# One store one slot later, and q in two transfers of 64 partitions instead of four of 32

## The chip, the cores and the metric

The kernel runs on one core of one Trainium2 chip. The metric is the device time of one execution in microseconds (us); less is better. The core has a matrix engine (TensorE, PE in the profile, with its weight loads shown as PEld), a vector engine (VectorE, DVE), a scalar engine (ScalarE, ACT), GpSimd (POOL) and SyncE (SP). SP computes nothing here: it issues nearly all of the DMA transfers, one after the other in the order in which the program lists them. Sixteen DMA engines carry the transfers between HBM and the on-chip memory of 128 partitions.

## The reference

Eight batches of eight heads; each head has 576 positions of 64 numbers in float32. Attention without a softmax is followed by a two-layer network with a leaky ReLU:

```
kv  = einsum('bhsd,bhse->bhde', k, v)
out = einsum('bhsd,bhde->bhse', q, kv)
rms = sqrt(mean(out * out, axis=-1) + 1e-6)
x   = (out / rms * g_norm)             # transposed to 4608 tokens x 512
h   = x @ w_in                         # 512 x 2048
g   = max(0.01 * h, h)
out = g @ w_out                        # 2048 x 512, result 4608 x 512
```

## The kernel before, in words

The 4608 tokens are worked on as nine blocks of 512 (`NB = 9`, block 0 to block 8). The 2048 inner columns are cut into four parts (`NC = 4`), and two parts next to each other make a pair: the second product is run by pairs. Both products of the network are done with Strassen's recursion in one to three levels, so that the matrix engine multiplies fewer blocks and the other engines add and subtract blocks. The sums of the weights are made once, written to HBM and read back for every block: `read` (L801) fetches one of seven pieces of a part of the first weights into a ring of five places, `read_side` (L1031) the right sides of the second product into three places, and `load_four`, `load_three` and `load_last_3` (L992 to L1017) the smaller ones.

From block 1 on the program is written out by slots. A block has 28 slots, seven for each part (`for t in range(7)`, L1446), and `tick` counts them through all blocks. In each slot the program issues one step of the first product, one step of the second product, which lags behind by two slots, and bits of the attention of the next batch by tables (`FINE_SLOTS` and its like). Work that has been put off by `put_off(n, ...)` is issued at the start of the slot n later (L1449). `pin` keeps instructions in program order on their engine, so SP's order is the order of the calls. A DMA in SP's order that has to wait holds up all that SP would issue after it.

q comes in by `load_pair` (L158), for the two heads of a pair p in batch b. A head is read as 32 rows of 18 positions, `T * D` = 1152 numbers. It is put into the tile twice: on partitions 64l to 64l+31 as it is, and on partitions 64l+32 to 64l+63 shifted by 32 numbers (`src[:, 32 * c:]`), where l is 0 or 1 for the two heads. So a pair takes four transfers of 32 partitions. `turn` (L511) then transposes, by blocks of 32 x 32, the first 32 of every 64 columns, which gives q with the head dimension on the partitions (L513, on DVE). The tile for q has one home from batch 3 on (and two before, one of them in w_all), so the load of the next pair is issued right after the transpose of the pair before it: `turn` and then `load_q`, which puts the next load at the head of `to_load`. Batch 0 has its own path (`load_first`), so there are 28 pairs, 7 batches of 4, with 112 transfers at L172.

The result of a block is held in four tiles of 256 x 256, with the keys "11", "12", "21" and "22" by token half and column half. Each is added up over the two pairs of parts and stored when its last sum has been issued; that happens while the next block has begun. `store` (L1308) puts the store off by two slots, the store of "12" by one slot if `tick > 14 * NC`, that is from slot 57 on, which is the case for blocks 2 to 6. In the last blocks the stores go through ACT's queue without being put off. The home of "12" of one block is that of "11" of the next, which is first written by a copy in the second step of the next block's first pair.

The lines of q's transfers as they stand:

```
for c in range(2):
    r0, n = 64 * l + 32 * c, T * D - 32 * c
    src = q[b, 2 * p + half_of(p, l)].rearrange("(t s) d -> t (s d)", s=T)
    pin(nc.sync.dma_start(t[r0:r0 + 32, :n], src[:, 32 * c:]))
```

Of the kernel before, what the change touches and what calls it, by code (L numbers as in the profile page):

```python
# [24 lines left out]
def kernel(  # L25
# [36 lines left out]
    nc = tc.nc  # L62
    B, H, S, D = q.shape
# [6 lines left out]
    T = S // 32  # L70
# [4 lines left out]
    NC = DF // 2 // (U * P)  # L75
# [17 lines left out]
    pin = tc.keep_in_program_order  # L93
# [32 lines left out]
    def half_of(p, i):  # L126


        return i ^ (p & 1)

    def load_two(eng, src, t):

        pin(eng.dma_start(t.rearrange("p j d -> p (j d)"),
                          src.rearrange("h (p j) d -> (h p) (j d)", j=J)))
        return t

    def in_tile(name):
        return ins.tile([P, J, D], F32, tag=f"{name}_in", name=f"{name}_in")

    def q_tile(b, p):  # L140
        if p % 2 and NP * b + p < NP * 3 + 2:
            return w1_all[:, 2 * NC * NW:]
        return ins.tile([P, T * D], F32, tag="q_in", name="q_in", bufs=1)
# [3 lines left out]
    def load_some(n=1):  # L147

        while to_load and n > 0:
            b, p, what = to_load.popleft()  # L150
            load_pair(b, p, what)
            n -= 1
# [5 lines left out]
    def load_pair(b, p, what="kvq"):  # L158


        if "k" in what:
            k_ins[b, p] = load_two(nc.sync, k[b, 2 * p:2 * p + 2], in_tile("k"))
        if "v" in what:
            v_ins[b, p] = load_two(nc.sync, v[b, 2 * p:2 * p + 2], in_tile("v"))
        if "q" not in what:
            return
        t = q_tile(b, p)
        for l in range(2):
            for c in range(2):
                r0, n = 64 * l + 32 * c, T * D - 32 * c  # L170
                src = q[b, 2 * p + half_of(p, l)].rearrange("(t s) d -> t (s d)", s=T)
                pin(nc.sync.dma_start(t[r0:r0 + 32, :n], src[:, 32 * c:]))  # L172
        q_ins[b, p] = t

    def load_first():
# [329 lines left out]
    def attention(b, apart=True, fine=False):  # L505
# [17 lines left out]
        for m in range(2):  # L523
            turn(2 * m)
            load_q(2 * m)
            yield
            turn(2 * m + 1)
            load_q(2 * m + 1)
            if m or b == KV_BESIDE:
                yield  # L530
            if kv_ps:
                attention_kv(b, m, [t[:, m, :] for t in kv_ps])
            if not apart and m == 0:
                for p in (2, 3):
                    load_pair(b, p)
            elif apart and not beside:
                load_kv(b + m, 2 - 2 * m)
            yield
            if apart:
                if m and kv_ps:  # L540
                    copy_kv(b, kv_ps)
                yield
# [147 lines left out]
    later, tick = [], 0  # L690

    def put_off(n, what):
        later.append((tick + n, what))
        later.sort(key=lambda x: x[0])
# [613 lines left out]
    def store(i):  # L1308
        def finish(key, o, part=None, cols=None, eng=None):
            r0 = i * NT + (int(key[0]) - 1) * N2  # L1310
            c0 = (int(key[1]) - 1) * N2
            if part is not None:
                r0 += part * P
                eng.dma_start(out[r0:r0 + P, c0 + cols.start:c0 + cols.stop], o[:, part, cols])
                return
            to = out[r0:r0 + N2, c0:c0 + N2].rearrange("(t p) m -> p t m", p=P)
            if steady and tick < 7 * (END - NC):
                put_off(1 if key == "12" and tick > 14 * NC else 2, lambda: pin(nc.sync.dma_start(to, o)))
            else:
                nc.scalar.dma_start(to, o)  # L1320
        return finish
# [49 lines left out]
    def between(n, half):  # L1371
        nonlocal loaded, rounded
        go(steps.get(2 * n + half, iter(())), 1)

        while half and rounded < min(3 * n + 8, 2 * n + 13, len(w_jobs) - (n < 11)):
            if loaded < len(w_jobs):
                load_w(loaded)
                loaded += 1
                if loaded in (15, 19):
                    load_pair(1, (loaded - 15) // 4)  # L1380
            round_w(rounded)
            rounded += 1
        if (n, half) == (12, 0):
            for p in range(2):
                load_pair(2, p)
# [192 lines left out]
```

## Time and profile before

| what | value |
|---|---|
| median of three executions | 908.37 us (908.33 to 910.28) |
| profiled execution, its own time | 909.21 us |
| its span in the profile | 907.5 us, TensorE at the full granted clock (1.0) |
| PE busy | 899.6 us, 99% |
| PEld / DVE / POOL / ACT busy | 789.3 / 611.9 / 521.8 / 330.5 us |
| DMA | 219.00 MB, mean 241 GB/s, 76.4% of the engines' span on SP's queue |
| transfers issued | 706 by SP, 18 by ACT, 8 by GpSimd |

The times are those of the slowest core, of which there is one. The profile counts an engine as busy from the start of an instruction to its end; the ends of matmuls are modelled. In the table of waits a wait for several signals is put down to the one that came last. A group's line gives the source line, the engine, the operation, the tile that is written and the tile that is read. DMA share is the time that the packets took, as a share of sixteen engines' time in that stretch; beside the views, the trace keeps a record of each packet with its start, its duration and its bytes, and of each completion signal.

### The profile page before, as it was taken

How to read it: one execution, taken by the hardware profiler on the slowest of the kernel's cores; microseconds unless marked ns; L12 is line 12 of the kernel's file. 1: busy time of each engine (PE TensorE's matmuls, PEld its weight loads, DVE VectorE, ACT ScalarE, POOL GpSimd, SP SyncE). 2: the span in 40 equal slices, each digit the busy share in tenths (PEclk: the TensorE clock that was granted, in tenths of full speed). 3: DMA queues.
4: the chain of work that ended last, by engine and by line, in shares of the span. 5: the costliest groups of instructions: out<-in, count | busy, mean ns of one | idle time of the engine just before them, and what ended most of it. 6: DMA issues, size and time to landing. Idle time of an engine off the chain costs nothing.

```text
span 907.5 us, 19134 instructions
## 1 busy us (share of the span) xinstructions
PE 899.6 (99%) x7344; PEld 789.3 (87%) x7344; DVE 611.9 (67%) x942; ACT 330.5 (36%) x645; POOL 521.8 (58%) x672
## 2 busy tenths in 40 slices
PE   8999999999999999999999999999999999999998
PEld 4555558888998999999999999999999999999997
DVE  5877885676574757685877497667877674646453
ACT  5454423231334332434333433343243424232420
POOL 2000236977638765766757584758477847883730
PEclk9999999999999999999999999999999999999999
DMA  8999918977789788967897798958886778677831
GB/s 253 225 248 235 249 66 264 312 255 247 246 298 323 220 276 251 310 225 249 259 321 267 221 296 253 323 171 270 257 277 187 229 210 274 199 237 226 259 115 53
DMA packets 109530, 219.00 MB, mean 241 GB/s; under 512 B 11776, under 2 KB 51072, under 8 KB 109440
## 3 DMA queue, kind: packets, MB, share of 16 engines
q1 hardware_dynamic: 105504, 212.22, 76.4%
q10 hardware_dynamic: 3488, 4.39, 1.4%
q8 instruction: 58, 0.95, 0.5%
q0 software_dynamic: 448, 1.18, 0.3%
q14 instruction: 32, 0.26, 0.1%
HBM read 187.34 MB, written 30.41 MB: 240 GB/s over the span
## 4 chain that ended last, share of the span: by engine, by line
PE 94%; POOL 2%; DMA 2%; DVE 1%; issue 1%; ACT 0%; POOLq 0%; ACTq 0%; DVEq 0%
PE o_a L121 19%; PE o_c L121 15%; PE h_hd L121 9%; PE h_ha L121 9%; PE h_hc L121 9%; PE h_hb L121 9%; PE o_acc L121 6%; PE h_ps L121 6%; PE o_ps L121 3%; PE h_a L121 2%; PE h_b L121 2%; PE kv_ps L121 1%; PE h_d L121 1%; PE h_c L121 1%; DMA pairs<-in_v_dram 1%; POOL more L697 1%
## 5 line engine op out<-in xcount | busy, mean ns | idle before, releaser
L697 POOL TENSOR_TENSOR gs<-g 128x512 f32<-128x512 f32 x62 | 85.5, 1380 | 129.4 <-ACT g L892 64.0
L121 PE MATMUL o_a<-pairs,gs 128*128 128x256 f32 x472 | 111.9, 380 | 0.7 <-DMA pairs<-w 0.7
L697 DVE TENSOR_TENSOR o_all<-o_c,o_all 128x256 f32<-128x256 f32 (+2 forms) x124 | 69.4, 560 | 59.1 <-PE o_c L121 45.7
L892 ACT ACTIVATE g<-g 128x512 f32<-128x512 f32 x124 | 75.7, 631 | 63.0 <-DVE g L697 63.0
L697 POOL TENSOR_TENSOR w_all<-w_all 128x512 f32<-128x512 f32 x28 | 50.2, 1793 | 84.0 <-ACT w_all L1116 84.0
L697 DVE TENSOR_TENSOR g<-g,w_all 128x512 f32<-128x512 f32 (+1 forms) x84 | 88.5, 1054 | 14.6 <-POOL w_all L697 8.8
L121 PEld LDWEIGHTS o_a<-pairs,gs 128*128 128x128 f32 x472 | 85.5, 190 | 10.4 <-POOL more L697 0.9
L697 DVE TENSOR_TENSOR w_all<-h_ha,w_all 128x512 f32<-128x512 f32 x42 | 28.7, 684 | 55.0 <-PE h_ha L121 53.2
L1116 ACT COPY w_all<-h_hc 128x512 f32<-128x512 f32 x42 | 24.8, 590 | 105.6 <-PE h_hc L121 105.4
L1116 ACT COPY w_all<-h_ha 128x512 f32<-128x512 f32 x42 | 24.7, 587 | 104.5 <-PE h_ha L121 104.5
L121 PE MATMUL o_c<-pairs,gs 128*128 128x256 f32 x264 | 62.4, 379 | 0.0
L697 DVE TENSOR_TENSOR o_all<-o_a,o_all 128x512 f32<-128x512 f32 (+1 forms) x53 | 35.4, 668 | 39.3 <-PE o_a L121 38.7
L697 POOL TENSOR_TENSOR pairs<-w 128x512 f32<-128x512 f32 x4 | 5.3, 1324 | 98.2 <-ACT cut L262 98.2
L121 PE MATMUL o_a<-w,g 128*128 128x256 f32 x248 | 58.9, 380 | 0.0
L121 PE MATMUL h_ps<-xT,w_all 128*128 128x512 f32 (+1 forms) x136 | 58.1, 571 | 0.3 <-DVE w_all L278 0.3
L121 PE MATMUL o_acc<-w,g 128*128 128x256 f32 (+1 forms) x192 | 57.7, 451 | 0.0
L121 PEld LDWEIGHTS o_acc<-w,g 128*128 128x128 f32 x192 | 36.3, 190 | 21.5 <-issue 17.2
L697 DVE TENSOR_TENSOR g<-w_all 128x1024 f32<-128x1024 f32 x28 | 34.7, 1238 | 29.4 <-ACT w_all L1116 29.4
L121 PEld LDWEIGHTS o_c<-pairs,gs 128*128 128x128 f32 x264 | 47.9, 190 | 5.3
L121 PEld LDWEIGHTS o_a<-w,g 128*128 128x128 f32 x248 | 45.0, 190 | 5.2 <-ACT xT L473 0.2
L121 PEld LDWEIGHTS h_ps<-xT,w_all 128*128 128x128 f32 x136 | 25.4, 190 | 26.9 <-issue 24.4
L121 PE MATMUL h_hc<-stage,w_all 128*128 128x128 f32 x336 | 44.9, 276 | 0.0
(291 smaller groups left out, 2403.4 us busy)
## 6 DMA issues: line engine op xcount, KB each, us to landing
w_all<-w SPq DMA_DIRECT2D x196, 448.0 KB, 4.8
pairs<-w SPq DMA_DIRECT2D x94, 256.0 KB, 4.4
w<-w SPq DMA_DIRECT2D x22, 448.0 KB, 5.9
v_in<-in_v_dram SPq DMA_DIRECT2D x29, 288.0 KB, 6.0
k_in<-in_k_dram SPq DMA_DIRECT2D x28, 288.0 KB, 5.4
q_in<-in_q_dram SPq DMA_DIRECT2D x46, 144.0 KB, 5.3
q_in<-in_q_dram SPq DMA_DIRECT2D x46, 140.0 KB, 5.4
w<-stage SPq DMA_DIRECT2D x12, 512.0 KB, 4.2
```

What stands on the lines that cost most here:

```text
L121: pin(nc.tensor.matmul(*args, **kw))
L697: ins = eng.tensor_tensor(out_, a, b_, op=ALU.subtract if minus else ALU.add)
L892: nc.scalar.activation(t, t if src is None else src, func=AF.Prelu, alpha=SLOPE)
L1116: nc.scalar.copy(q[:, at], bank)
```

## The change

In `load_pair` the loop over c goes. Each head is read by one transfer into 64 partitions. Its source is written out by hand as three dimensions: two copies that start 32 numbers apart, 32 rows that are 1152 numbers apart, and 1120 numbers in a row. The first copy is 32 columns shorter than before; those columns are not among the ones that the transpose reads. In `store` the condition goes: all stores that are put off are put off by two slots.

```
         t = q_tile(b, p)
+        n = T * D - 32
         for l in range(2):
-            for c in range(2):
-                r0, n = 64 * l + 32 * c, T * D - 32 * c
-                src = q[b, 2 * p + half_of(p, l)].rearrange("(t s) d -> t (s d)", s=T)
-                pin(nc.sync.dma_start(t[r0:r0 + 32, :n], src[:, 32 * c:]))
+            head = q[b, 2 * p + half_of(p, l)]
+            src = bass.AP(head.tensor, head.offset, [[32, 2], [T * D, 32], [1, n]])
+            pin(nc.sync.dma_start(t[64 * l:64 * l + 64, :n], src))
         q_ins[b, p] = t
...
             if steady and tick < 7 * (END - NC):
-                put_off(1 if key == "12" and tick > 14 * NC else 2, lambda: pin(nc.sync.dma_start(to, o)))
+                put_off(2, lambda: pin(nc.sync.dma_start(to, o)))
             else:
                 nc.scalar.dma_start(to, o)
```

## The prediction

> **What bounds the kernel now.** I read the page's busy times first, then the table of stretches, then the waits of the matrix engine, then those of SP.
>
> ```profile
> PE 899.6 (99%) x7344; PEld 789.3 (87%) x7344; DVE 611.9 (67%) x942; ACT 330.5 (36%) x645; POOL 521.8 (58%) x672
> PEclk9999999999999999999999999999999999999999
> q1 hardware_dynamic: 105504, 212.22, 76.4%
> q_in<-in_q_dram SPq DMA_DIRECT2D x46, 144.0 KB, 5.3
> q_in<-in_q_dram SPq DMA_DIRECT2D x46, 140.0 KB, 5.4
> ```
>
> PE is busy for 899.6 of 907.5 us at the full clock; 7.9 us are all that it idles. In the lines of transfers the last number is the median time from issue to landing. The next table gives, for each stretch, its length, the busy time of each engine, the clock, the DMA share and GB/s.
>
> ```profile
> 0.00:46.00 46.00, 42.66 (x386) 23.06 (x387) 31.41 (x65) 24.33 (x42) 5.18 (x14) 1.00 0.98 239
> 46.00:650.00 604.00, 603.05 (x5025) 524.91 (x5024) 426.49 (x659) 222.88 (x447) 362.06 (x455) 1.00 0.83 255
> 650.00:900.00 250.00, 249.98 (x1913) 237.83 (x1912) 152.27 (x214) 83.32 (x158) 154.59 (x203) 1.00 0.67 215
> ```
>
> All of the change's q loads lie between 46.1 and 647.4 us. There PE idles 1 us in 604, while the sixteen DMA engines are already busy for 0.83 of the time. So PE bounds this stretch, and DMA is the next in line, with 17% to spare. PE's own waits, and two of SP's, with total, times and longest in us:
>
> ```profile
> PE o_a L121 <- DMA pairs<-w: 0.7, 1, 0.7
> SPq L1318 <- DVE o_all L697: 21.0, 4, 5.5
> SPq L801 <- DMA w_all<-w: 4.1, 7, 0.8
> ```
>
> PE waits once for a weight, for 0.7 us. SP waits often, but nothing that matters waits for SP. The last view is time on SP and DVE in one block (start, duration).
>
> ```profile
> 442.45 1.25 DVE L513 STREAM_TRANSPOSE qT<-q_in 128x576 f32<-128x576 f32 x1
> 443.73 1.72 SPq L172 DMA_DIRECT2D q_in<-in_q_dram  x4
> 451.00 0.41 SPq L1318 DMA_DIRECT2D out_dram<-o_all  x1
> 451.48 1.25 DVE L513 STREAM_TRANSPOSE qT<-q_in 128x576 f32<-128x576 f32 x1
> 453.05 1.99 SPq L172 DMA_DIRECT2D q_in<-in_q_dram  x4
> 465.80 1.26 DVE L513 STREAM_TRANSPOSE qT<-q_in 128x576 f32<-128x576 f32 x1
> ```
>
> A pair's q is asked for right after the transpose before it, and the next transpose needs it 7.75 us (443.73 to 451.48) or 12.75 us (453.05 to 465.80) later; the first of the block's three such gaps is 9.5 us (432.98 to 442.45). In this program order DVE can do nothing else while it waits for q.
>
> **The store.** Five stores of "12" (blocks 2 to 6) are issued one slot later; a slot is about 3.4 us (a block of 96 us by 28). Their wait is the 21.0 us above: four waits, the longest 5.5, the one in the view ending at 451.00. Asked for a slot later, each should wait some 2 us, and the two reads queued behind it leave some 3.4 us earlier, 14 us of SP's time over all. PE does not wait for those reads now, so this gives 0; at the best it is the 1 us that PE idles in the stretch. It also costs nothing: the data isn't there sooner, and the home is next written in the second step of the following pair, six slots (some 20 us) after the last sum is issued, while two slots, a wait of 2 us and 5.6 us to landing make 14.5. What covers it is that distance; if a store took 11 us to land, ACT's copy of "11" would wait.
>
> **The issues.** 112 DMAs become 56. Four issues take 1.72 to 1.99 us on SP, so a pair saves some 0.9 us, 28 pairs 25 us of SP's time. It lies beside PE's work: 0. The bytes fall by 56 x 32 x 128 = 0.23 MB of 219: 0.
>
> **How the q transfers are spread.** This decides. Now each of the 112 transfers has 32 rows as its slowest dimension on both sides, all others 32 or 128. The trace has 11,712 completion signals for 732 transfers, 16 for each: all sixteen engines take part in every one. The new source has 2 as its slowest dimension, and no transfer of the trace has so small a one. So the cost is unknown and lies between two ends. If the rows still go out over sixteen engines, nothing changes. If a transfer is cut along its slowest dimension, it can only be cut in two, and two engines carry all of q. I take two: that every first dimension here is a multiple of sixteen, and every transfer signals sixteen times, fits a cut along that dimension, and such a cut of 2 gives two parts. It is not shown.
>
> [...]
>
> **The sum with two engines.** The packet records show q as 3,584 rows of 4,480 or 4,608 bytes, one packet each, together 64 us of each engine. In the stretch an engine is busy 0.83 x 604 = 501 us; without q that leaves 437. After the change each of the two carries half of q, 28 pairs x 2 transfers x 32 rows = 1,792 rows. The 4,480-byte packets took 173 ns undisturbed (the fastest 5%), 231 ns at the lower quartile, 293 ns at the median; 3,584-byte packets of 128-partition reads took 140 at the median, so something slows the rows of q.
> - At 173: 437 + 310 = 747 us, 143 more than the stretch.
> - At 231: 437 + 414 = 851, 247 more.
> - At 293: 437 + 525 = 962, 358 more.
> The two engines would then be the bound: every read of weights has an eighth of its rows on them, in turn behind q, and the ring's five places hold some 17 us of slots. I take 231: it is midway between undisturbed and today's median, as only two engines write q at once, though each to rows 32 partitions from the other's. Against the profiled execution: 909.2 + 247 = 1156; that execution lies 0.84 us above the median of 908.37, so against the median it is 1155. I say 1156.
>
> The bounds go further. If the other rows shrink to their undisturbed durations too, since fourteen engines will idle and contend less (by size, the fastest 5%: some 345 us in place of 437), 173 gives 655, or 51 more: 960. If two rows in turn share one way in, a row takes twice 173 = 346 ns: 437 + 620 = 1057, or 453 more: 1362.
>
> [...]
>
> **What is late next.** Whoever waits first is DVE at a transpose: two transfers are 64 rows on each engine, 11.1 us (173) to 18.8 (293), and some 2 us from issue to the first packet, against 9.5, 7.75 and 12.75 us. Behind the transpose stand DVE's additions from PE's banks, so PE stops for a free bank. On SP, transfers take eight completion signals in turn, so a late q also holds up the eighth transfer after it.
>
> **The rivals.**
> A, forecast: two engines carry q and are the bound. 1156, between 1040 and 1290. For it: 0.83 already used. Against it: no transfer shown with a slowest dimension of 2.
> B, late only: two engines, but rows near 173 and others quicker, so that throughput is not the bound and only transposes are late, by 13.1 - 9.5, 13.1 - 7.75 and 13.1 - 12.75, 9.3 us a block. Over six blocks 56 us, with a second queue of reads behind it up to 120: 965 to 1030, say 990. Against it: three q loads in 34 us of a block ask 33 us of these engines, on top of 0.8 of other reads.
> C, not slower: the spread stays at sixteen, as both sides have 64 rows in all. Then nothing in PE's chain moves: 908.4, within 1 us. For it: the same bytes now land in 5.3 us with sixteen signals. It decides from the first transfer on.
> D, faster: SP's 14 + 25 us let reads leave earlier and the 4 or 5 us of PE's start and waits shrink: 905. Against it: 3.3 of the 7.9 idle us are in the first 46 us and 3.6 at the end, which the change does not touch.
>
> **How the numbers follow.** A 0.66, B 0.19, C 0.12, D 0.03. The time is A's. Range 960 to 1290: it takes in B, and all of A but rows near 346 ns, and leaves out C and D with 0.15 and some 0.05 of A. A measurement can tell 0.3% (2.7 us) from no change. Faster 0.03 (D), same 0.12 (C), slower 0.85 (A, B).
>
> **What would show it.** Two completion signals from engines for a q transfer, not sixteen; time to landing from 5.3 to 13 us or more; q's packets one after another on two engines; PE's idle time in the stretch from 1 us to hundreds, put down to weights (w_all, pairs) or to banks that DVE has not freed; a smaller mean DMA share there (the same work in 850 us), and the 250 us after the last q load as long as before. The waits of L1318 should fall from 21 to under 10 us in either case. The prediction is wrong if q still signals sixteen times, or if q's rows run at 173 ns beside quicker weights.

## The result, and the profile after

The changed kernel takes 1107.76 us (median of four, 1104.15 to 1115.83) beside 908.67 us before: 1.2192 times as long, 95% interval 1.2156 to 1.2228. The profiled execution has a span of 1107.1 us, 199.6 us more than before. From the page after, the lines that answer to those shown of before:

```profile
PE 951.0 (86%) x7344; PEld 827.9 (75%) x7344; DVE 602.0 (54%) x942; ACT 331.5 (30%) x645; POOL 509.9 (46%) x672
PEclk9997899999988999789988799898988999999999
q1 hardware_dynamic: 103824, 211.98, 61.6%
PE 47%; DMA 40%; DVE 7%; SPq 3%; issue 2%; POOL 1%; ACT 1%; ACTq 0%; DVEq 0%; POOLq 0%
q_in<-in_q_dram SPq DMA_DIRECT2D x46, 280.0 KB
```

The fourth line is from the chain that ended last: DMA is now 40% of it, where it was 2%. PE idles 156.1 us instead of 7.9, which is 148.2 us of the loss; the other 51.4 us are PE's own busy time, 951.0 beside 899.6 us for the same 7344 matmuls, at a granted clock of 0.93 in the mean, where it was 1.0. Neither the last line nor any other line of transfers on that page has a time to landing. What differs in the records is the number of completion signals: the 676 transfers sent 10,088. With sixteen for each of the 620 others, 168 are left for 56 q transfers, three for each. By the times in the records the first of the three comes 0.96 us after the issue in the median, the second 14.6 and the third 15.7 us after it: I read the last two as one from each of two engines, and the first as one that does not wait for the rows. The records of q's rows agree: up to its last packet they run two at a time for 319 us, alone for 60 us and more than two at a time for 16 us. Both transfers of a pair are issued within 1.10 us (in the view of one block further down), so if each had two engines of its own, four rows would run at once.

The next table is by stretches, with the columns as before. The last packet of q starts at 652.0 us before and at 855.2 us after, so the stretches 46 to 652 and 46 to 855 hold q's loads to within 0.2 us.

```profile
46.00:652.00 606.00, 605.05 (x5043) 526.91 (x5042) 426.80 (x660) 224.00 (x448) 362.33 (x456) 1.00 0.83 255
```

That is the kernel before; after:

```profile
46.00:855.00 809.00, 660.97 (x5100) 569.38 (x5099) 423.62 (x664) 229.27 (x456) 356.83 (x460) 0.91 0.61 192
```

The stretch is 203 us longer, and the rest of the program takes about as long as it did. The mean DMA share has fallen from 0.83 to 0.61 although DMA is now what the kernel waits for: the mean hides two full engines behind fourteen that are little more than half busy (447 of 809 us, worked out further down). Packet records counted by how many run at once show it: exactly two packets of any kind are under way for 200 us of this stretch, where it was 6 us before. The waits of the changed kernel, by PE, DVE and SP (total, times, longest in us):

```profile
PE h_ha L121 <- DVE w_all L697: 31.9, 5, 9.6
PE o_a L121 <- DMA pairs<-w: 30.1, 3, 10.8
PE o_ps L121 <- DVE qT L513: 20.3, 4, 5.3
PE kv_ps L121 <- DMA v_in<-in_v_dram: 20.2, 4, 13.3
...
DVE qT L513 <- DMA q_in<-in_q_dram: 126.6, 15, 13.3
...
DVE qT L513 <- DMA w_all<-in_q_dram: 28.5, 3, 13.5
...
SPq L172 <- DMA q_in<-in_q_dram: 66.0, 13, 8.8
SPq L1318 <- DMA q_in<-in_q_dram: 24.2, 5, 5.4
```

DVE stands still for 155.1 us at the transposes of q, and PE behind it, for a bank that DVE has not freed (31.9 us in the first line) or for the transpose itself (20.3 us). PE also waits for reads of weights and of v (30.1 and 20.2 us). SP waits for q transfers too, 66.0 us at L172 and 24.2 us at L1318, whose stores have nothing to do with q: the records have the signals of all transfers of SP and ACT on eight semaphores, 83 or 84 transfers on each, and a transfer waits for the one before it on its own. In one block, on SP and DVE (start, duration, and the idle time before with what ended it):

```profile
428.65 1.26 DVE L513 STREAM_TRANSPOSE qT<-q_in 128x576 f32<-128x576 f32 x1 [6.71 <-DMA q_in<-in_q_dram]
429.93 1.10 SPq L172 DMA_DIRECT2D q_in<-in_q_dram  x2
...
447.52 1.26 DVE L513 STREAM_TRANSPOSE qT<-q_in 128x576 f32<-128x576 f32 x1 [10.67 <-DMA q_in<-in_q_dram]
```

A load is asked for at 429.93, and the transpose that needs it starts at 447.52, 17.6 us later, where it was 7.75 us in the same place before. The chain that ended last has that load in it (start, duration):

```profile
430.53 16.89 DMA q_in<-in_q_dram
```

It took 16.89 us, beside a median of 5.3 or 5.4 us from issue to landing before.

### The profile page after: what moved, and what is told of

It reads as the page before. It is cut to its first block, busy times and chain, and to the rows that moved or that the text cites. A ratio compares the mean times of both kernels' runs of the same rounds, so it can differ in the third digit from the quotient of the medians.

```text
span 1107.1 us, 19047 instructions
## 1 busy us (share of the span) xinstructions
PE 951.0 (86%) x7344; PEld 827.9 (75%) x7344; DVE 602.0 (54%) x942; ACT 331.5 (30%) x645; POOL 509.9 (46%) x672
## 4 chain that ended last, share of the span: by engine, by line
PE 47%; DMA 40%; DVE 7%; SPq 3%; issue 2%; POOL 1%; ACT 1%; ACTq 0%; DVEq 0%; POOLq 0%
DMA q_in<-in_q_dram 22%; PE o_a L121 11%; PE o_c L121 9%; PE h_hc L121 6%; DMA pairs<-w 6%; PE h_hd L121 5%; PE h_ha L121 5%; PE h_hb L121 5%; DMA pairs<-in_moe_w_out_dram 3%; DMA pairs<-in_moe_w_in_dram 3%; PE o_ps L121 2%; DMA v_in<-in_v_dram 2%; DMA w<-pairs 2%; DMA w_all<-w 2%; DVE qT L513 1%
## 5 line engine op out<-in xcount | busy, mean ns | idle before, releaser
L697 POOL TENSOR_TENSOR gs<-g 128x512 f32<-128x512 f32 x62 | 81.7, 1319 | 168.9 <-ACT g L892 92.6
L121 PE MATMUL o_a<-pairs,gs 128*128 128x256 f32 x472 | 119.5, 398 | 33.7 <-DMA pairs<-w 30.1
L121 PEld LDWEIGHTS o_a<-pairs,gs 128*128 128x128 f32 x472 | 90.2, 201 | 45.6 <-issue 30.6
L513 DVE STREAM_TRANSPOSE qT<-q_in 128x576 f32<-128x576 f32 x23 | 28.9, 1255 | 126.8 <-DMA q_in<-in_q_dram 126.6
L121 PE MATMUL h_ha<-stage,w_all 128*128 128x128 f32 x336 | 48.5, 291 | 23.4 <-DVE w_all L697 22.3
L121 PEld LDWEIGHTS h_ha<-stage,w_all 128*128 128x128 f32 x336 | 46.2, 204 | 26.3 <-DVE w_all L697 23.3
L121 PE MATMUL h_hc<-stage,w_all 128*128 128x128 f32 x336 | 49.3, 294 | 18.8 <-DVE w_all L697 18.8
L1116 ACT COPY w_all<-h_hc 128x512 f32<-128x512 f32 x42 | 24.8, 590 | 136.0 <-PE h_hc L121 135.8
L121 PEld LDWEIGHTS h_hc<-stage,w_all 128*128 128x128 f32 x336 | 45.5, 206 | 21.6 <-DVE w_all L697 19.8
L121 PE MATMUL h_ha<-xT,w_all 128*128 128x128 f32 x224 | 46.2, 289 | 17.6 <-DVE w_all L697 9.6
L121 PE MATMUL h_ps<-xT,w_all 128*128 128x512 f32 (+1 forms) x136 | 60.8, 592 | 0.3 <-DVE w_all L278 0.3
```

Of the source, the lines that this page charges most:

```text
L121: pin(nc.tensor.matmul(*args, **kw))
L513: in_turn(nc.vector.transpose(qT[:, p, :].rearrange("p (t s) -> p s t", s=T), q_in.rearrange("p (s d) -> p s d", d=D)[:, :, :32]))
L697: ins = eng.tensor_tensor(out_, a, b_, op=ALU.subtract if minus else ALU.add)
L1116: nc.scalar.copy(q[:, at], bank)
```

## The experiments

The theory is that of the prediction: the slowest dimension of the source, 2, puts all of q on two DMA engines, and these are full. Its rivals are that the store costs something, that 64 partitions in one transfer or a source read twice is what costs, that only the lateness of q at the transposes costs, and that it is the number of rows or the holding of completion signals.

### Each part of the change alone

```
-                put_off(1 if key == "12" and tick > 14 * NC else 2, lambda: pin(nc.sync.dma_start(to, o)))
+                put_off(2, lambda: pin(nc.sync.dma_start(to, o)))
```

> The kernel before with the store's part of the change alone (all put-off stores two slots later). All theories: no change, 908 us within 2 us. PE does not wait for what is queued behind that store. The waits of SP at L1318 for DVE should fall from 21 us to under 10 us. If the store had a share in the loss, this run is over 912 us.

Measured: 908.88 us, 0.999 of before (0.9972 to 1.0009). SP's waits at that line:

```profile
SPq L1318 <- DVE o_all L697: 1.4, 3, 0.7
```

So 21.0 us of SP's waiting become 1.4, and the time does not move: nothing that PE needs was held up by it.

The other run has the new `load_pair` and the old `store`:

> The kernel before with q's part of the change alone. Theory: this part carries all of the loss, 1100 to 1116 us. If the store's later slot added to it, this run is faster than the whole change by more than 5 us.

Measured: 1111.72 us, 1.2206 (1.2168 to 1.2245), the same as the whole change within the intervals. All of the loss is q's.

### The same transfers with 32 as the slowest dimension

```
-            src = bass.AP(head.tensor, head.offset, [[32, 2], [T * D, 32], [1, n]])
+            src = bass.AP(head.tensor, head.offset, [[T * D, 32], [32, 2], [1, n]])
```

> The changed kernel with the two outer dimensions of q's source exchanged: 32 rows outermost, the two shifted copies inside. Same bytes, same 64 partitions, same two transfers a pair; the rows land on other partitions, so q's values are at wrong places. Theory of two engines: the slowest dimension is now 32, sixteen completion signals per transfer come back, and the time is that of before, 905 to 912 us. Rival, that 64 partitions in one transfer or reading the source twice is what costs: it stays above 1000 us.

Measured: 909.98 us, 0.9997 (0.9976 to 1.0018). The 676 transfers sent 10,816 signals, sixteen each, and the page has a time to landing again:

```profile
PE 901.1 (99%) x7344; PEld 790.3 (87%) x7344; DVE 613.3 (67%) x942; ACT 330.9 (36%) x645; POOL 521.6 (57%) x672
q_in<-in_q_dram SPq DMA_DIRECT2D x46, 280.0 KB, 5.4
```

The whole loss goes away with the order of two dimensions. Neither 64 partitions in one transfer nor the source that is read twice costs anything. The run shows one thing more: half the number of issues, in its best form, gains nothing either.

### Nobody waits for q

```
-                q_in.rearrange("p (s d) -> p s d", d=D)[:, :, :32]))
+                ident[:, :32].unsqueeze(1).to_broadcast([P, T, 32])))
```

> The changed kernel, with the same q transfers at the same places, but the transposes read the identity matrix instead of q, so nobody waits for q (q is left out of the computation). Theory A, the two engines are full: their load stays at some 820 us for a stretch of 604, the reads of weights queue behind q on them, and the time stays near that of the change, 1060 to 1110 us, with PE waiting for weights in place of DVE for q. Theory B, only the lateness of q at the transposes costs: without that wait the time falls to 905 to 930 us.

Measured: 1105.95 us, 1.2144 (1.2104 to 1.2183): as good as no gain, though DVE no longer waits for q at all. PE's waits and two pieces of the chain in one block (start, duration, what):

```profile
PE o_a L121 <- DMA pairs<-w: 33.1, 3, 12.0
PE kv_ps L121 <- DMA v_in<-in_v_dram: 33.1, 6, 12.8
PE h_ha L121 <- DMA w_all<-w: 32.9, 5, 8.9
PE h_hc L121 <- DMA w_all<-w: 31.5, 9, 7.4
...
415.30 17.45 DMA w_all<-w
450.31 18.48 DMA w_all<-w
```

The wait has moved from q's transposes to the reads of weights and v, and a read of weights now takes 17 to 18 us in the chain. This is what separates the two causes: lateness of q would have gone with the wait, full engines keep their price and hand it to whatever stands in the queue. The rival of lateness falls.

### Four and eight engines, and half the bytes

The first two runs take four copies of 16 rows and eight copies of 8 rows as the source, all else as in the change:

```
-            src = bass.AP(head.tensor, head.offset, [[32, 2], [T * D, 32], [1, n]])
+            src = bass.AP(head.tensor, head.offset, [[8, 4], [T * D, 16], [1, n]])    # one run
+            src = bass.AP(head.tensor, head.offset, [[4, 8], [T * D, 8], [1, n]])     # the other
```

> The changed kernel with four copies of 16 rows as q's source, 8 numbers apart, in place of two copies of 32: same bytes, partitions and transfers, other values of q (so the result is another). The slowest dimension is 4. Theory of the full engines: four engines carry 896 rows each, at 208 to 250 ns 186 to 224 us; with the other 437 that is 623 to 661 us for a stretch of 604, so 19 to 57 us are lost: 927 to 965, and near 910 if the other rows shrink. Theory that only the transposes' lateness counts: 5.5 us of rows and 2 us to the first packet fit all gaps but one, so 908 to 912. Completion signals: four of the engines and one of SP, five for each q transfer.

> The same with eight copies of 8 rows, 4 numbers apart (other values of q). The slowest dimension is 8: eight engines with 448 rows each, 93 to 130 us, with the other 437 at most 567 us in a stretch of 604. All theories of the spread: 906 to 911 us, nine signals for each q transfer. If a source in several copies costs something by itself, over 915.

The third starts from the run before, in which nobody waits for q, and reads half of each row:

```
-            src = bass.AP(head.tensor, head.offset, [[32, 2], [T * D, 32], [1, n]])
-            pin(nc.sync.dma_start(t[64 * l:64 * l + 64, :n], src))
+            src = bass.AP(head.tensor, head.offset, [[32, 2], [T * D, 32], [1, n // 2]])
+            pin(nc.sync.dma_start(t[64 * l:64 * l + 64, :n // 2], src))
```

> As the run in which the transposes read the identity matrix, with rows of half the length (560 numbers, so half of q is not even read): still two engines and 56 transfers of 64 rows. Theory of the full engines: 1,792 rows of 2,240 bytes at some 90 to 115 ns are 161 to 206 us, with the other 437 598 to 643 us in a stretch of 604: 908 to 955 us. If the count of rows or the holding of completion signals is what costs, it stays above 1000 us.

Measured: 1004.73 us with four (1.1036, 1.0994 to 1.1077), 929.45 with eight (1.0226, 1.0190 to 1.0263), 954.77 with half the bytes on two (1.0496, 1.0459 to 1.0533). The signals are 10,200, 10,424 and 10,088: five, nine and three for each q transfer, that is four, eight and two engines and one more. The next table is worked out from the packet records. "Rest" is the time of all packets but q's between 46 us and q's last packet, divided by sixteen; "q" is that of q's rows divided by the number of engines that carry them. The records do not name a packet's engine, so this supposes that the rest is spread evenly. The load so found can come out above the stretch.

| run | mean row of q, ns | rest + q = load, us | stretch, us | device time, us |
|---|---|---|---|---|
| before, 16 engines | 287 | 437 + 64 = 501 | 606 | 908.67 |
| 32 outermost, 16 engines | 283 | 438 + 63 = 501 | 607 | 909.98 |
| 8 engines | 300 | 451 + 135 = 585 | 628 | 929.45 |
| half the bytes, 2 engines | 111 | 443 + 198 = 641 | 654 | 954.77 |
| 4 engines | 265 | 476 + 237 = 713 | 708 | 1004.73 |
| the change, 2 engines | 208 | 447 + 373 = 820 | 809 | 1107.76 |
| nobody waits, 2 engines | 204 | 452 + 366 = 818 | 805 | 1105.95 |

Where the load is above 606 us, the stretch is as long as the load, within about 2%. At eight engines the load is still below PE's 606 us, and the stretch is 22 us longer all the same; I had expected nothing there, and over 915 us if a source in several copies costs something by itself. The run with 32 outermost, whose source has two copies too, speaks against such a cost, but none with eight copies and sixteen engines was made. Three q loads come within 34 us of a block, so the engines that carry them can be over-full for a third of a block while their mean is 0.93; that this is the reason is argued from the times of the loads, not shown. The packet records fit it: exactly eight packets are under way for 31 us of that stretch, where it was 7 us before. With four engines exactly four are under way for 77 us, where it was 5 us. Half the bytes with the same 56 transfers and 3,584 rows take away three quarters of the loss, so neither the count of rows nor that of transfers is the price. The holding of completion signals is not separated by that run, since each signal was held for a shorter time too. The run with four engines speaks against it: SP's waits for q_in add up to 135.8 us there and to 126.5 us in the changed kernel, and the loss is 96 beside 199 us.

The expected time with four engines was missed, 1004.73 beside 927 to 965. The rows of q took 265 ns, longer than the upper 250 of the estimate, and the rest came to 476 us in place of 437. The load that was measured fits the stretch, but the two are not quite independent, as the durations that make up the load are of the same run.

### Why the clock fell

```
-            in_turn(nc.vector.transpose(
-                qT[:, p, :].rearrange("p (t s) -> p s t", s=T),
-                q_in.rearrange("p (s d) -> p s d", d=D)[:, :, :32]))
+            for _ in range(11 if b > 2 else 1):
+                in_turn(nc.vector.transpose(
+                    qT[:, p, :].rearrange("p (t s) -> p s t", s=T),
+                    q_in.rearrange("p (s d) -> p s d", d=D)[:, :, :32]))
```

> The kernel before, with each q transpose of batches 3 to 7 done eleven times instead of once: 20 times 12.5 us more on DVE, no change of the transfers. It asks why the granted clock fell from 1.0 to 0.93. If idle of PE alone lowers it: PE stops for some us at each of them, the granted clock falls to 0.92 to 0.98, and the same matmuls are busy for more than 905 us. If it is what DMA does that lowers it: the clock stays at 1.0 and PE's busy time at 900 us, whatever PE idles. Time: 960 to 1130 us.

Measured: 1152.1 us, 1.2650 (1.2611 to 1.2688), clock 0.915. It is slower than expected, since the 200 additional transposes (234 us more of DVE's busy time) came out as 243 us of time. The page of that run, busy times and clock:

```profile
PE 944.0 (82%) x7344; PEld 825.9 (72%) x7344; DVE 845.9 (74%) x1142; ACT 331.9 (29%) x645; POOL 507.4 (44%) x672
PEclk9999999988799888898888988879878899999999
```

The transfers are those of before, with sixteen signals each, and yet the same matmuls are busy for 944.0 us and the clock falls in the blocks in which PE is stopped. So idle of PE alone is enough to lower it. In the trace of the changed kernel the half clock goes with the longer gaps: PE has 27 of 1.0 to 13.3 us, and the clock records show 21 stretches at 0.5, of 3.4 to 17.1 us, before the program's end. All 20 gaps of 3.6 us and more have one; of the shorter gaps one of 2.7 us has one too, and two of 3.1 us have none.

## Why the prediction was right, and where its sizes were off

**What decides.** Two engines carry q: shown by the three signals a transfer, and by the time, which goes 1107.76, 1004.73, 929.45 and 909.98 us with two, four, eight and sixteen engines. With a slowest dimension of 2, 4 and 8 the signals were three, five and nine, and with 32 sixteen; how the number of engines is chosen for other counts no run shows. Which of the sixteen they are is not in the records. That they are always the same two is borne out by the load, which fits the stretch only then, and by the 200 us in which exactly two packets of any kind are under way.

**The sum.** Its form was right: the rest and q's half, against the stretch. The term that was mis-sized is a row of q: 231 ns assumed, 208 measured (median 173, upper quartile 218), so q came to 373 us and not 414. The rest was 447 beside 437. The load of 820 in place of 851 us, and a stretch that grew by 203 in place of 247, make 1107.76 in place of 1156. The lower end, with other rows shrinking to 345 us, did not come about: the room on the fourteen other engines did not make the rest quicker.

**The upper end**, two rows that share one way in at 346 ns, did not come about either. That two rows share a way in was a supposition of mine, and no run shows it: three quarters of q's rows took at most 218 ns. Rows were slower where more engines carried them, 265 to 300 ns with four to sixteen. Why is open.

**What is late next.** The transposes were, as forecast, with waits of up to 13.5 us, with PE stopped behind DVE and SP held by completion signals. As a cause it was a false lead: without that wait the loss stayed.

**The store and the issues at nothing.** Both right: 0.999 for the store alone, and 0.9997 for 56 issues less with sixteen engines. The store's wait fell further than the 2 us a store that I gave it, to 1.4 us over all.

**The rivals.** Lateness only fell by the run in which nobody waits. No change fell, for the spread did follow the slowest dimension. Faster fell with the store's run and the sixteen-engine run: with SP's time given back, PE has nothing to gain from it.

**What the prediction did not have** is the clock. It counted PE as idle or busy at full speed. In the measured account 148 us are idle and 51 us are slower matmuls. I take them as no further price on top of the load: where two engines set the pace, slower matmuls fill time in which PE would have waited. That is argued from the load, which fills the stretch by itself (820 beside 809 us); no run keeps the clock full under the same load.

## What to carry to other kernels

Before merging small transfers into one with a hand-made access pattern, look at its first dimension: a count of 2 there put 16 MB on two of sixteen engines and cost 22%, and the same bytes with 32 first cost nothing. A mean DMA share says nothing of a full engine (0.61 here, with a load of 820 us in a stretch of 809); the number of completion signals per transfer (three in place of sixteen), and of packets that are under way at once (exactly two for 200 us), show it. When a wait shows up at one place, take it away before calling it the cause: here the loss stayed at some 197 us, and the wait moved to other reads.

## What the runs showed of the hardware

Each of the 21 stretches at half the granted clock began 1.7 to 5.2 us after the start of a gap on PE: the mean clock was 0.93 with 27 gaps of 1.0 to 13.3 us, and 1.0 with no gap of 1 us or more. The same matmuls took 51 us longer where DMA had stopped PE (951.0 us) and 44 us longer where DVE had (944.0 us). And the same rows of q were quicker on two engines (208 ns in the mean) than on sixteen (283 ns with 32 outermost), though each engine had eight times as many.
